# One core, attention and soft mixture: the first batch's casts, z parts, bounds and x times u stand at other places, and with them the last batch's v, three logits and the shifts

## Chip, cores and metric

The kernel runs on one core of a Trainium2 chip. The metric is the device time of one execution in microseconds, as the median of several.

## What is computed

Eight batches of relu-squared attention, followed by one soft mixture of experts over all tokens (cut to what matters):

```python
# u, v: (8, 2496, 256)   z: (8, 2496, 64)   f32
scores = (1/2496) * z @ z.transpose(0, 2, 1)
attn = np.maximum(scores, 0.0) ** 2
x = (u * (attn @ v)).reshape(19968, 256)
# phi: (256, 32)   w1: (8, 256, 1024)   w2: (8, 1024, 256)
logits = x @ phi
d = softmax(logits, axis=0)          # over tokens
slot_in = d.T @ x                    # 32 slots, 4 to an expert
slot_out[e] = relu(slot_in[e] @ w1[e]) @ w2[e]
out = softmax(logits, axis=1) @ slot_out
```

## The kernel before

**Halves.** A batch's 2496 queries are cut into five chunks, its keys into ten pieces of 256. One chunk with one piece is a half; a batch has 50, numbered through from 0. Matrices that need accuracy are held as two f16 parts, a high and a low one. For half k, `prepare(k)` issues: on TensorE the scores `sc` (z of the keys with z of the queries), on ScalarE relu and square into `r`, on GpSimd or ScalarE the cast `ph` (high part), on VectorE `pl`, which is r minus ph (low part). Since the scores are symmetric, VectorE also transposes `r` into `y`, and SyncE's DMAs carry it through DRAM, so that the mirrored half later only loads its `r`. Then `sums_halves` multiplies ph and pl by v into the accumulator `acc`, in two phases; between the phases stands `prepare` of a later half, and with it that half's scores. At the end of a chunk, `finish_chunk` multiplies the accumulator by u into `xg`.

**Order.** Every engine takes its instructions in the order in which the program writes them (`keep_in_program_order`). The order is written by hand: `landing[h]` holds what is issued with half h, and runs at the end of a `prepare`; tables say which step has which h. `work` holds the steps of the mixture for 1024 tokens (logits, exponentials, block transpositions, four shifts by DMA, the combine weights `c0` to `c3`); one is taken out with each half from the third piece of a chunk on.

**z, bounds, v.** The first 12 halves take their scores from raw f32 z. From half 14 on (halves 12, 13 are mirrored) they take z's two parts: `load_z` gives `split`, ScalarE's high part and then VectorE's low part. Scores consist of three pairs of matmuls: high with high, high keys with low queries, low keys with high queries. In batch 0, `FIRST_Z` says with which half each of z_1 to z_4 is split; scores 14 and 15 need z_1 and z_2, scores 16 and 17 z_1 and z_4, scores 18 first need z_3. For a later batch z's scale comes from its bounds: a square with a maximum per block (`sq`, into `tops`), summed over partitions by two small matmuls on TensorE (`add_bounds`), then `factors`. v's scale comes from its `energy` by `largest` (two VectorE instructions, into `few`) and `scale_v`, which begins with a small matmul on TensorE. v then is split like z (`v_high`, `v_low`).

**Opening.** Halves 0 and 1 are summed in f32, halves 2 and on in parts. In what comes first, GpSimd casts `r` of half 2 as soon as ScalarE has squared it, while VectorE runs `largest`; half 3 comes from an ordinary `prepare(3)` later.

Of the kernel before, what the change touches and what calls it, by code (L numbers as in the profile page):

```python
# [8 lines left out]
F32 = mybir.dt.float32  # L9
# [9 lines left out]
P = 128  # L19
B, S, D, DQK = 8, 2496, 256, 64  # L20
# [5 lines left out]
QC = 512  # L26
NQ = 5
# [4 lines left out]
NP = KT // 4  # L32
NBLK = 16
NRAW = 12
NW_OWN = 7
# [10 lines left out]
)  # L46
FIRST_MEETS = ((0, 1, 2, 3, 4), (1, 0, 2, 4, 3)) + MEETS[0][2:]

FIRST_Z = {8: 1, 10: 2, 11: 4, 13: 3}

RAW_SCORES = 12

FILL = 6, 3

WHOLE, KEEP = 2, 6

ON_ACT = 3, 5, 7

# [25 lines left out]
def attn_soft_moe_kernel(ctx, tc, uT, v, zz, zh, phi, ww, outT):  # L84
    nc = tc.nc

    pe, act, dve, sp, gp = (InOrder(tc, x) for x in (nc.tensor, nc.scalar, nc.vector, nc.sync, nc.gpsimd))
# [82 lines left out]
    def add_bounds(b, ps, js):  # L170
        ones_k = nc.const_aps.tensor(1.0, [P, P], F32)
        for h, rows in enumerate(HALF if b else [slice(0, P)]):
            pe.matmul(ps[:, h, js], ones_k[rows], tops[b % 2][rows, js], start=True, stop=True)

    def factors(b, ps, js):


        n2, by = (t[b % 2][:, js] for t in (norm2, z_by))
        total = ps[:, 0, js]
        if b:  # L180
            dve.tensor_reduce(n2, ps[:, :, js].rearrange("p h j -> p j h"), axis=AX.X, op=ALU.add)
            total = n2
        dve.tensor_scalar(bits(n2), bits(total), EVEN, None, op0=ALU.bitwise_and)
        dve.tensor_scalar(
            bits(by), bits(n2), EVEN, 1, op0=ALU.bitwise_xor, op1=ALU.logical_shift_right
        )
        dve.tensor_scalar_mul(by, by, 2.0**77)
# [29 lines left out]
    def largest(b):  # L217


        root, w = v_by[b % 2], few[b % 2]  # L220
        n2 = norm2[b % 2].unsqueeze(2).to_broadcast([P, NP, 2])
        dve.tensor_scalar(
            bits(root), bits(energy[b % 2]), 1, ROOT, op0=ALU.logical_shift_right, op1=ALU.bitwise_and
        )
        r2 = root.rearrange("p (j i) -> p j i", i=2)
        dve.tensor_tensor_reduce(
            r2, r2, n2, 1.0, 2.0**-120, op0=ALU.mult, op1=ALU.max, accum_out=w[:, 0:1]
        )

# [72 lines left out]
    own_w = moe.enter_context(tc.tile_pool(name="own_w", bufs=1))  # L302
    turns_sb = moe.enter_context(tc.tile_pool(name="turns_sb", bufs=4))
    att = ExitStack()
    wa = att.enter_context(tc.tile_pool(name="wa", bufs=2, side="right"))

    ut_ = {}
# [53 lines left out]
    middle, behind, stores, turning, casting, splitting = [], [], [], [], [], []  # L361

    def run(todo):
        now, todo[:] = todo[:], []
        for f in now:
            f()
# [99 lines left out]
    def prepare_first(k):  # L466

        r = wa.tile([P, 2, QC], F32, tag="r", name=f"r_{k}", bufs=4)
        pend[k] = hi, lo = high_low(k)
        ps, _ = early.pop(k)  # L470

        def parts(t):
            nc.gpsimd.tensor_copy(hi[:, t], r[:, t])
            return lambda: dve.tensor_sub(lo[:, t], r[:, t], hi[:, t])

        return lambda: relu(k, r, ps), lambda: act.activation(r, r, AF.Square), parts, lambda: stage(k, r)
# [119 lines left out]
    def await_(x, y):  # L596
        tc.add_manual_dep(
            x.ins, y.ins.name,
            mybir.DependencyInfo(mybir.DependencyClass.Sync, mybir.DependencyReason.DATA),
            reason="bank",  # L600
        )
# [64 lines left out]
    xg_ = {}  # L666

    def finish_chunk(b, ch, acc):
        j, _, n, t0 = ch
        ut = ut_.pop(t0)  # L670
        s = 0
        while s < n:
            q, o = divmod(t0 + s, 1024)
            w = min(n - s, 1024 - o)
            if q not in xg_:
                xg_[q] = wk.tile([P, 2, 1024], F32, tag="xg", name=f"xg_{q}")
            for c in (slice(0, 1), slice(1, 2)) if t0 + n == N else (slice(0, 2),):
                first = t0 == 0
                dve.scalar_tensor_tensor(
                    xg_[q][:, c, o : o + w], acc[:, c, s : s + w], out_by[b % 2][:, j : j + 1],  # L680
                    kept[0][:, c] if first else ut[:, c, s : s + w],
                    op0=ALU.mult, op1=ALU.add if first else ALU.mult,
                )
                if first:
                    dve.tensor_mul(xg_[q][:, :, 0:w], xg_[q][:, :, 0:w], ut)
            if o + w == 1024:
                work.extend(groups(q))
            s += w
# [23 lines left out]
    def groups(q):  # L712
# [3 lines left out]
        x = xg_[q]  # L716
# [134 lines left out]
        blocks = [lambda j=j, c=c: behind.append(lambda: turn_block(j, c)) for j in range(2) for c in range(2)]  # L851
# [3 lines left out]
        rest = lambda: None  # L855
        if q < NQG - 2:

            todo = [logits, ex, *blocks, e, *shifts[0:2], c0, *shifts[2:4], c1, c2]
            todo.append(lambda: (c3(), late.append(slot_sums)))
        else:  # L860


            todo = [rest, rest, logits, ex, lambda: behind.append(adding.pop(0)), rest]
            todo += [c0, c1, c2, c3, turn_e_whole, *[lambda i=i: turn_x_whole(i) for i in range(4)]]
            todo.append(lambda: late.append(last_slot_sums))
        return todo

    parts = {}
# [78 lines left out]

    def load_u(b, ch):
        _, _, n, t0 = ch
        ut = wa.tile([P, 2, QC], F32, tag="ut", name=f"ut_{t0}", bufs=1)  # L950
        q0 = t0 - b * S
        sp.dma_start(
            ut[:, :, :n], uT[b, :, q0 : q0 + n].rearrange("(c p) q -> p c q", p=P)
        )
        ut_[t0] = ut

    work = []
# [4 lines left out]
    for b in range(1, B):  # L962
        base, order = (b - 1) * 2 * NP * NQ, BLOCKS[b == B - 1]
        z_at = [28, 29, 30, 31, 39]
        v_from = [6, 7, 8, 9, 24, 25, 26, 31, 32, 33]
        v_sq = [17, 18, 19, 20, 28, 29, 30, 32, 33, 33]
        v_high = [43, 41, 41, 42, 42, 43, 44, 44, 45, 45]
        v_low = [47, 42, 43, 44, 45, 46, 48, 49, 50, 51]
        for i, (j, at) in enumerate(zip(order, z_at)):
            splits.setdefault(base + 9 + 2 * i, []).append((load_z, b, j, [base + 12 + 2 * i, base + at]))  # L970
        for i, (start, *steps) in enumerate(zip(v_from, v_sq, v_high, v_low)):
            splits.setdefault(base + start, []).append((load_v, b, i, [base + at for at in steps]))
        later[base + 23] = lambda b=b: add_bounds(b, next_acc(), slice(0, NP))
        later[base + 24] = lambda b=b: factors(b, accs[-1], slice(0, NP))
        later[base + 36] = lambda b=b: largest(b)
        later[base + 39] = lambda b=b: scale_v(b, ms_ps.tile([P, 2, 512], F32, tag="ms", name=f"mx_{b}"))
    landing, fetched = {}, set()
    accs = []

    def next_acc():  # L980

        accs.append(acc_ps.tile([P, 2, QC], F32, tag="acc", name=f"acc_{len(accs)}"))
        return accs[-1]
# [86 lines left out]
    for i in range(2, 2 * NP):  # L1070
        first_v[i](act if i in ON_ACT else dve)
    square2()
    low2 = [parts2(t) for t in range(2)]
    largest(0)
    sums_raw(1, acc_raw, 0, [1])
    scale_v(0, small)
    sums_raw(1, acc_raw, 1)
# [8 lines left out]
    dve.tensor_scalar(  # L1086
        raw_by[:, NP:], z_by[0][:, 1:2], z_by[0][:, 1:2], 2.0**-22, op0=ALU.mult, op1=ALU.mult
    )
    prepare(3)
    kept = [own_w.tile([P, 2, QC], F32, tag="own", name="kept", bufs=NW_OWN)]  # L1090
    landing_kept = lambda: act.activation(kept[0], acc_raw, AF.Identity, scale=2.0**22 / S**2)
    landing[KEEP] = [landing_kept]
# [1 line left out]
    for h, x in enumerate(halves):  # L1094
        if h < WHOLE:
            continue
        if x.begins:
            chunk = h // (2 * NP)
            acc = accs[chunk] if chunk < len(accs) else next_acc()
        last = len(halves) - h  # L1100
        transfers(h)
        if work and (x.at > 1 or last <= 20):
            work.pop(0)()
        weights(last)
        behind.extend(landing.pop(h, ()))
        ahead = [k for k in range(h + 2 + (h > CATCH), h + 3 + (h >= CATCH)) if k < len(halves) and k >= 3]
        split_first_v()
        run(casting)
        if not ahead and h < 1:
            run(middle)  # L1110
            run(turning)
            run(behind)
            sums_halves(h, acc, 1, sums_halves(h, acc, 0, None))
        elif ahead and not halves[ahead[0]].turned:
            turn = sums_halves(h, acc, 0, None)
            prepare(ahead.pop(0))
            sums_halves(h, acc, 1, turn)
        else:
            if ahead and not x.ends:
                prepare(ahead.pop(0))  # L1120
            elif not ahead:
                run(middle)
                run(casting)
                run(splitting)
                run(behind)
                between_last(3 - last)
            sums_whole(h, acc)
        if x.ends:
            finish_chunk(x.b, x.ch, acc)
        for k in ahead:  # L1130
            prepare(k)
        if h in FIRST_Z:
            z_splits.pop(FIRST_Z[h])()
        del pend[h]
# [314 lines left out]
```

## Time and profile before

| | us |
|---|---|
| median of 3 runs | 1269.56 |
| lowest, highest | 1269.4, 1270.18 |
| the profiled execution | 1269.41 |
| its span | 1267.6 |
| its mean granted TensorE clock | 0.987 of full speed |
| busy: VectorE | 1046.0 |
| busy: ScalarE | 841.9 |
| busy: GpSimd | 229.3 |
| tail with the outputs' DMAs at 417 GB/s | from about 1220 to the end |

The span runs from the first to the last instruction of the profiled execution; 1.8 us of its time lie outside. Busy times are sums over the span, so they say nothing of where an engine is needed; that is read from single stretches.

### The profile page before, as it was taken

The page shows a single profiled execution, that of the slowest core. Times are in us where ns is not written, and L with a number is a line of the kernel's source. Part 1 is how long each engine was busy: PE and PEld are TensorE (multiplying, and loading weights), DVE is VectorE, ACT ScalarE, POOL GpSimd, SP SyncE. Part 2 cuts the span into 40 slices and gives each one's busy share as a digit, 9 for nine tenths or more (in the row PEclk, how much of TensorE's full clock was granted, in tenths as well). Part 3 has the DMA queues.
Part 4 walks back from the last instruction along what each step waited for, and adds up shares of the span by engine and source line. Part 5 has one row for each costly group of instructions (what it writes and reads, how often), then busy time and mean ns, then how long its engine had stood idle before and what let it go on. Part 6 is the DMA issues. An engine that isn't in the chain of part 4 may idle for free.

```text
span 1267.6 us, 27769 instructions
## 1 busy us (share of the span) xinstructions
PE 1241.6 (98%) x10936; PEld 604.5 (48%) x10937; DVE 1046.0 (83%) x1468; ACT 841.9 (66%) x1143; POOL 229.3 (18%) x234
## 2 busy tenths in 40 slices
PE   9999999999999999999999999999999999999984
PEld 3444454444544444445544444444444455445752
DVE  7988898779978889788987888788987789776563
ACT  7877765767666766577656776577666777564552
POOL 2211032201311032110311123110321113110100
PEclk9999999999999999999999999999999999999995
DMA  6778469773878748784787758786587848989769
GB/s 197 244 211 277 170 190 303 232 238 119 240 263 270 240 126 274 244 235 163 213 276 218 268 149 244 256 255 210 156 277 230 267 142 239 277 278 328 280 272 376
DMA packets 136690, 299.28 MB, mean 236 GB/s; under 512 B 17904, under 2 KB 38896, under 8 KB 124656
## 3 DMA queue, kind: packets, MB, share of 16 engines
q1 hardware_dynamic: 136560, 297.51, 74.0%
q8 instruction: 86, 1.41, 0.5%
q14 instruction: 44, 0.36, 0.1%
HBM read 162.43 MB, written 113.77 MB: 218 GB/s over the span
## 4 chain that ended last, share of the span: by engine, by line
PE 93%; ACT 2%; DVE 2%; DMA 1%; issue 1%; POOL 0%; ACTq 0%; DVEq 0%; POOLq 0%
PE acc L80 76%; PE sc L80 11%; PE lg L80 3%; DMA outT<-ot 1%; PE pf L80 1%; ACT r L80 1%; ACT ot L80 1%; DVE pl L80 1%; PE h L80 1%; PE po L80 0%; DVE y L80 0%; PE acc_raw L80 0%; DVE v L80 0%; DVE xg L80 0%; PE xt L80 0%
## 5 line engine op out<-in xcount | busy, mean ns | idle before, releaser
L80 PE MATMUL acc<-ph,v 64*128 64x512 f16 (+4 forms) x5004 | 923.7, 368 | 0.4 <-POOLq L80 0.3
L80 PEld LDWEIGHTS <-v 64*128 64x128 f16 (+1 forms) x7506 | 467.7, 95 | 521.3 <-issue 38.6
L80 PE MATMUL acc<-pl,v 64*128 64x512 f16 (+5 forms) x2502 | 597.9, 368 | 2.3 <-DVE pl L80 2.3
L80 DVE TENSOR_TENSOR pl<-r,ph 128x1024 f16<-128x1024 f32 (+1 forms) x428 | 475.7, 1123 | 35.0 <-ACT ph L80 25.6
L80 POOL CAST ph<-r 128x1024 f16<-128x1024 f32 (+1 forms) x210 | 224.4, 1072 | 942.7 <-ACT r L80 693.8
L80 ACT ACTIVATE r<-sc 128x1024 f32<-128x1024 f32 (+1 forms) x233 | 220.3, 946 | 234.5 <-PE sc L80 231.9
L80 DVE STREAM_TRANSPOSE y<-r 128x1024 f32<-128x1024 f32 x160 | 198.3, 1239 | 68.9 <-ACT r L80 65.0
L80 ACT ACTIVATE r<-r 128x1024 f32<-128x1024 f32 (+1 forms) x243 | 239.0, 983 | 7.7
L80 ACT CAST ph<-r 128x1024 f16<-128x1024 f32 (+1 forms) x180 | 172.0, 963 | 98.3 <-PE acc L80 60.0
L80 PE MATMUL sc<-z,z 64*128 64x512 f16 x912 | 123.9, 376 | 0.0
L80 PEld LDWEIGHTS <-z 64*128 64x128 f16 x1380 | 69.7, 94 | 72.1 <-DVE z L80 0.3
L80 DVE SCALAR_TENSOR_TENSOR xg<-acc,out_by,ut 128x1024 f32<-128x1024 f32 (+7 forms) x56 | 50.6, 926 | 17.7 <-PE acc L80 17.4
L80 DVE SCALAR_TENSOR_TENSOR v<-vr,v_by,v 128x512 f16<-128x512 f32 (+1 forms) x81 | 60.6, 750 | 0.0
L80 ACT ACTIVATE v<-vr,v_by 128x512 f16<-128x512 f32 (+1 forms) x81 | 53.8, 707 | 7.6 <-DVE v_by L80 7.6
L80 DVE STREAM_TRANSPOSE yd<-r 128x512 f32<-128x512 f32 x36 | 25.5, 709 | 31.2 <-ACT r L80 29.8
L80 PE MATMUL sc<-z 64*128 64x512 f16 (+1 forms) x468 | 50.6, 321 | 0.0
L80 DVE STREAM_TRANSPOSE y<-xg 128x512 f32<-128x512 f32 x72 | 49.4, 686 | 0.0
L80 ACT ACTIVATE vq<-vr 128x512 bf16<-128x512 f32 x73 | 45.5, 623 | 3.6 <-DMA vr<-in_v 3.3
L80 DVE COPY ot<-pf 128x1024 f32<-128x1024 f32 (+2 forms) x21 | 24.1, 1147 | 18.1 <-PE pf L80 14.6
L80 DVE TENSOR_TENSOR pl<-rd,ph 128x512 f16<-128x512 f32 x36 | 24.7, 686 | 14.9 <-ACT ph L80 14.9
L80 ACT COPY ot<-pf 128x1024 f32<-128x1024 f32 (+2 forms) x21 | 20.0, 951 | 22.8 <-PE pf L80 16.4
L80 DVE SCALAR_TENSOR_TENSOR z<-zr,z_by,z 128x512 f16<-128x512 f32 x35 | 25.8, 737 | 0.0
(193 smaller groups left out, 555.9 us busy)
## 6 DMA issues: line engine op xcount, KB each, us to landing
turned<-y SPq DMA_DIRECT2D x320, 256.0 KB, 5.5
r<-turned SPq DMA_DIRECT2D x76, 1024.0 KB, 7.3
xt<-y SPq DMA_DIRECT2D x288, 72.0 KB, 3.9
vr<-in_v SPq DMA_DIRECT2D x80, 256.0 KB, 4.9
outT<-ot SPq DMA_DIRECT2D x17, 1024.0 KB, 7.0
ut<-in_uT SPq DMA_DIRECT2D x31, 512.0 KB, 6.2
lent<-yd SPq DMA_DIRECT2D x144, 64.0 KB, 3.3
rd<-lent SPq DMA_DIRECT2D x36, 256.0 KB, 4.0
```

The source lines that it names most:

```text
L80: return lambda *a, **k: self.tc.keep_in_program_order(f(*a, **k))
```

## The change

It does six things, all of them in the order of instructions.

1. Opening: ScalarE takes relu and square of half 3 directly behind the square of half 2, ahead of v's high parts. GpSimd's first cast waits for the second instruction of `largest`, and half 3's two casts follow half 2's.
2. `FIRST_Z`: z_1, z_2, z_4 and z_3 are split with halves 10, 11, 13 and 15, where 8, 10, 11 and 13 stood. The first chunk's product of x and u is not issued in `finish_chunk` but with half 17; the first u lies in another buffer.
3. Batch 1's five squares of the bounds stand with halves 21 to 25 (12, 14, 16, 18, 20 before), its `add_bounds` with half 26 (23 before), its `factors` with 27 (24).
4. Some of the last batch's low parts of v come up to four halves earlier.
5. In batches 1, 3 and 5 the logits are taken out of `work` one half earlier.
6. `c0` stands behind all four shifts, no longer between the second and the third, so the last two shifts come earlier.

```diff
-FIRST_Z = {8: 1, 10: 2, 11: 4, 13: 3}
+FIRST_Z = {10: 1, 11: 2, 13: 4, 15: 3}
+FIRST_U = 17
+EDGE = 21
...
-        def parts(t):
-            nc.gpsimd.tensor_copy(hi[:, t], r[:, t])
+        def parts(t, behind_of=None):
+            cast = gp.tensor_copy(hi[:, t], r[:, t])
+            if behind_of is not None:
+                await_(cast, behind_of)
             return lambda: dve.tensor_sub(lo[:, t], r[:, t], hi[:, t])
...
                 if first:
-                    dve.tensor_mul(xg_[q][:, :, 0:w], xg_[q][:, :, 0:w], ut)
+                    landing.setdefault(FIRST_U, []).append(
+                        lambda x=xg_[q][:, :, 0:w]: dve.tensor_mul(x, x, ut)
+                    )
...
-            todo = [logits, ex, *blocks, e, *shifts[0:2], c0, *shifts[2:4], c1, c2]
+            todo = [logits, ex, *blocks, e, *shifts, c0, c1, c2]
...
-        v_low = [47, 42, 43, 44, 45, 46, 48, 49, 50, 51]
+        v_low = [47, 42, 43, 44, 45, 46, 48, 49, 50, 51] if b < B - 1 else [46, 42, 43, 43, 44, 44, 45, 45, 46, 47]
         for i, (j, at) in enumerate(zip(order, z_at)):
-            splits.setdefault(base + 9 + 2 * i, []).append((load_z, b, j, [base + 12 + 2 * i, base + at]))
+            bound = 21 + i if b == 1 else 12 + 2 * i
+            splits.setdefault(base + 9 + 2 * i, []).append((load_z, b, j, [base + bound, base + at]))
...
-        later[base + 23] = lambda b=b: add_bounds(b, next_acc(), slice(0, NP))
-        later[base + 24] = lambda b=b: factors(b, accs[-1], slice(0, NP))
+        add_at = 26 if b == 1 else 23
+        later[base + add_at] = lambda b=b: add_bounds(b, next_acc(), slice(0, NP))
+        later[base + add_at + 1] = lambda b=b: factors(b, accs[-1], slice(0, NP))
...
     square2()
-    low2 = [parts2(t) for t in range(2)]
-    largest(0)
+    relu3, square3, parts3, stage3 = prepare_first(3)
+    relu3()
+    square3()
+    found = largest(0)
+    low2, low3 = ([parts(t, found if parts is parts2 and t == 0 else None) for t in range(2)] for parts in (parts2, parts3))
     sums_raw(1, acc_raw, 0, [1])
...
-    prepare(3)
+    run(turning)
+    for f in low3:
+        f()
+    stage3()
...
-        if work and (x.at > 1 or last <= 20):
+        if work and (x.at > 1 or last <= 20 or (0 < x.b < B - 1 and h % (2 * NP * NQ) == EDGE)):
             work.pop(0)()
```

**The opening on GpSimd and ScalarE.** GpSimd before: the casts of half 2 (`ph_241`), then those of half 3 (`ph_287`) and of half 4.

```order
L473 CAST ph_241<-r_240 128x512 [waits Activation_49]
L473 CAST ph_241<-r_240 128x512
L80 CAST ph_287<-r_283 128x512 [waits Activation_49]
L80 CAST ph_287<-r_283 128x512
L80 CAST ph_318<-r_311 128x512 [waits PE_49,Activation_49]
```

GpSimd now, the same place; half 3's cast is `ph_262`:

```order
L84 CAST ph_241<-r_240 128x512 [waits DVE_49,Activation_49]
L84 CAST ph_241<-r_240 128x512
L84 CAST ph_262<-r_261 128x512 [waits Activation_49]
L84 CAST ph_262<-r_261 128x512
L84 CAST ph_318<-r_311 128x512 [waits PE_49,Activation_49]
```

ScalarE before, from the square of half 2 (`r_240`) on; `r_283` is half 3:

```order
L80 ACTIVATE r_240<-r_240 128x1024
L80 ACTIVATE v_2_127<-vr_2_134,v_by_89 128x256 [waits DMAHW5_49,DVE_49]
L80 ACTIVATE v_2_127<-vr_2_134,v_by_89 128x256
L80 ACTIVATE v_2_127<-vr_3_135,v_by_89 128x2x256
L80 ACTIVATE r_283<-sc_236,raw_by 128x1024 [waits PE_49]
L80 ACTIVATE r_283<-r_283 128x1024 [waits Activation_49]
```

ScalarE now; `r_261` is half 3:

```order
L84 ACTIVATE r_240<-r_240 128x1024
L84 ACTIVATE r_261<-sc_236,raw_by 128x1024 [waits PE_49]
L84 ACTIVATE r_261<-r_261 128x1024 [waits Activation_49]
L84 ACTIVATE v_2_127<-vr_2_134,v_by_89 128x256 [waits DMAHW5_49,DVE_49]
L84 ACTIVATE v_2_127<-vr_2_134,v_by_89 128x256
L84 ACTIVATE v_2_127<-vr_3_135,v_by_89 128x2x256
```

The first cast has a wait on VectorE more, and half 3's relu and square have moved ahead of v_2's three high parts.

**VectorE about halves 14 to 17.** Before, from z_4's low part on: `pl` and `y` of half 14 (`r_725`), a square of the bounds, `pl` and `y` of half 15 (`r_774`), and z_3's low part.

```order
L80 SCALAR_TENSOR_TENSOR z_4_125<-cw,z_by_85,z_4_125 128x512 [waits Activation_49]
L80 TENSOR_TENSOR pl_736<-r_725,ph_735 128x512 [waits PE_49,Activation_49]
L80 TENSOR_TENSOR pl_736<-r_725,ph_735 128x512 [waits Activation_49]
L80 STREAM_TRANSPOSE y_741<-r_725 128x2x16x32 [waits DMAHW3_49,DMAHW4_49,DMAHW2_49,DMAHW1_49]
L80 ISA sq_0_743,tops_82<-zr_0_533 128x512 [waits DMAHW6_49]
L80 ISA tops_82 128x1
L80 TENSOR_TENSOR pl_785<-r_774,ph_784 128x512 [waits PE_49,Activation_49]
L80 TENSOR_TENSOR pl_785<-r_774,ph_784 128x512 [waits Activation_49]
L80 STREAM_TRANSPOSE y_741<-r_774 128x2x16x32
L80 SCALAR_TENSOR_TENSOR z_3_124<-cw,z_by_85,z_3_124 128x512 [waits Activation_49]
L80 TENSOR_TENSOR pl_834<-r_823,ph_833 128x512 [waits PE_49,Pool_49]
L80 TENSOR_TENSOR pl_834<-r_823,ph_833 128x512 [waits Pool_49]
```

Now, from `y` of half 14 (`r_722`) on; `r_769` is half 15, `r_818` half 16, `r_865` half 17:

```order
L84 STREAM_TRANSPOSE y_738<-r_722 128x2x16x32 [waits DMAHW3_49,DMAHW4_49,DMAHW2_49,DMAHW1_49]
L84 TENSOR_TENSOR pl_780<-r_769,ph_779 128x512 [waits PE_49,Activation_49]
L84 TENSOR_TENSOR pl_780<-r_769,ph_779 128x512 [waits Activation_49]
L84 STREAM_TRANSPOSE y_738<-r_769 128x2x16x32
L84 SCALAR_TENSOR_TENSOR z_4_125<-cw,z_by_85,z_4_125 128x512 [waits Activation_49]
L84 TENSOR_TENSOR pl_829<-r_818,ph_828 128x512 [waits PE_49,Pool_49]
L84 TENSOR_TENSOR pl_829<-r_818,ph_828 128x512 [waits Pool_49]
L84 STREAM_TRANSPOSE y_834<-r_818 128x2x16x32 [waits DVE_49]
L84 TENSOR_TENSOR pl_876<-r_865,ph_875 128x512 [waits PE_49,Activation_49]
L84 TENSOR_TENSOR pl_876<-r_865,ph_875 128x512 [waits Activation_49]
L84 STREAM_TRANSPOSE y_834<-r_865 128x2x16x32
L84 SCALAR_TENSOR_TENSOR z_3_124<-cw,z_by_85,z_3_124 128x512 [waits DMAHW6_49,Activation_49]
```

z_4 has moved behind `y` of half 15, to where z_3 stood, and z_3 behind `y` of half 17; the square is gone from here.

TensorE before, at scores 16 (`sc_824`), between the two phases of half 14's sums:

```order
L80 MATMUL acc_667<-pl_736,v_4_128 128x512
L80 LDWEIGHTS z_4_125
L80 MATMUL sc_824<-z_1_122,z_4_125 128x512 [waits Activation_49]
L80 LDWEIGHTS z_4_125
L80 MATMUL sc_824<-z_1_122,z_4_125 128x512
L80 LDWEIGHTS z_4_125
L80 MATMUL sc_824<-z_1_122,z_4_125 128x512
L80 LDWEIGHTS z_4_125
L80 MATMUL sc_824<-z_1_122,z_4_125 128x512
L80 LDWEIGHTS z_4_125
```

TensorE now, the same place (`sc_819`):

```order
L84 MATMUL acc_664<-pl_733,v_4_128 128x512
L84 LDWEIGHTS z_4_125 [waits Activation_49]
L84 MATMUL sc_819<-z_1_122,z_4_125 128x512 [waits PE_49]
L84 LDWEIGHTS z_4_125
L84 MATMUL sc_819<-z_1_122,z_4_125 128x512
L84 LDWEIGHTS z_4_125
L84 MATMUL sc_819<-z_1_122,z_4_125 128x512
L84 LDWEIGHTS z_4_125
L84 MATMUL sc_819<-z_1_122,z_4_125 128x512
L84 LDWEIGHTS z_4_125 [waits DVE_49]
```

The weights for the first pair now wait for ScalarE's z_4 and those for the third pair for VectorE's.

**TensorE and VectorE at the bounds of batch 1.** TensorE before, at the end of scores 26 (`sc_1193`):

```order
L80 LDWEIGHTS z_3_124
L80 MATMUL sc_1193<-z_2_123,z_3_124 128x512
L80 LDWEIGHTS z_3_124
L80 MATMUL sc_1193<-z_2_123,z_3_124 128x512
L80 MATMUL acc_1207<-tops_82,const-float32-1.0 128x5 [waits DVE_49]
L80 MATMUL acc_1207<-tops_82,const-float32-1.0 128x5
```

TensorE now, at the end of scores 29 (`sc_1331`), which the second phase of half 26's sums follows:

```order
L84 LDWEIGHTS z_2_123
L84 MATMUL sc_1331<-z_2_123 128x256
L84 LDWEIGHTS z_2_123
L84 MATMUL sc_1331<-z_2_123 128x256
L84 MATMUL acc_1348<-tops_82,const-float32-1.0 128x5 [waits DVE_49]
L84 MATMUL acc_1348<-tops_82,const-float32-1.0 128x5
L84 LDWEIGHTS v_6_129 [waits Pool_sequencer_49]
L84 MATMUL acc_1035<-ph_1219,v_6_129 128x512
```

VectorE now, `y` of half 28 (`r_1285`) and what follows it; `y_1248<-xg_662` is a block's transposition:

```order
L84 TENSOR_TENSOR pl_1270<-r_1235,ph_1269 128x1024 [waits PE_49,Pool_49]
L84 STREAM_TRANSPOSE y_1246<-r_1285 128x2x16x32 [waits Activation_49]
L84 STREAM_TRANSPOSE y_1248<-xg_662 128x4x4x32
L84 ISA sq_4_1298,tops_82<-zr_4_850 128x512 [waits DMAHW2_49,DVE_49]
L84 ISA tops_82 128x1
L84 TENSOR_TENSOR pl_1315<-r_1285,ph_1314 128x1024 [waits PE_49,Pool_49]
```

The two small matmuls over `tops` have moved by three halves, and the last square stands behind two transpositions on VectorE, where before the second of those was followed by `pl`.

## Rows read from the trace of the kernel before

**Rows 1.** The first part of the page: busy time of an engine, its share of the span, and its number of instructions.

```profile
PE 1241.6 (98%) x10936; PEld 604.5 (48%) x10937; DVE 1046.0 (83%) x1468; ACT 841.9 (66%) x1143; POOL 229.3 (18%) x234
```

**Rows 2.** The fourth part of the page, its row by engine: what share of the span the chain of waits that ended last spends on each.

```profile
PE 93%; ACT 2%; DVE 2%; DMA 1%; issue 1%; POOL 0%; ACTq 0%; DVEq 0%; POOLq 0%
```

**Rows 3.** TensorE by stretches of the span: from and to, length, busy time and instructions, granted clock as a share of full speed, busy share of the DMA engines, GB/s.

```profile
700.00:1000.00 300.00, 300.00 (x2615) 1.00 0.75 230
...
1230.00:1240.00 10.00, 5.34 (x62) 0.79 1.02 417
1240.00:1250.00 10.00, 7.04 (x56) 0.50 1.01 419
```

**Rows 4.** What TensorE waited for over the whole span: us in total, number of waits, the longest.

```profile
PE acc L80 <- DVE pl L80: 2.3, 6, 0.8
PE acc L80 <- DVE few L80: 0.7, 1, 0.7
PE acc L80 <- POOLq L80: 0.3, 1, 0.3
```

**Rows 5.** The timeline of the opening and, for the last two of VectorE's rows, of a later batch: start and duration in us, engine, line and operation, with the idle time ahead of it and what ended it in brackets. First VectorE, then GpSimd, then TensorE.

```profile
13.87 0.44 DVE L80 TENSOR_SCALAR v_by<-energy 128x10 int32<-128x10 int32 x1
14.34 0.51 DVE L80 CUSTOM_DVE_ANT_1 v_by<-v_by,norm 128x10 f32<-128x10 f32 x1
...
20.60 1.06 DVE L80 TENSOR_TENSOR pl<-r,ph 128x512 f16<-128x512 f32 x1 [0.29 <-POOL ph L80]
...
129.73 0.17 DVE L80 TENSOR_SCALAR v_by<-energy 128x10 int32<-128x10 int32 x1
129.93 0.17 DVE L80 CUSTOM_DVE_ANT_1 v_by<-v_by,norm 128x10 f32<-128x10 f32 x1
...
13.66 1.17 POOL L473 CAST ph<-r 128x512 f16<-128x512 f32 x2 [9.95 <-ACT r L80]
19.95 1.17 POOL L80 CAST ph<-r 128x512 f16<-128x512 f32 x2 [5.11 <-ACT r L80]
...
15.01 0.46 PE L80 MATMUL acc<-ident,few 128*128 128x128 f32 x2 [0.74 <-DVE few L80]
```

**Rows 6.** The timeline of halves 11 to 14: VectorE, then TensorE.

```profile
50.06 1.22 DVE L80 TENSOR_TENSOR xg<-xg,ut 128x1024 f32<-128x1024 f32 x1
51.20 1.28 DVE L80 TENSOR_TENSOR pl<-r,ph 128x512 f16<-128x512 f32 x2
52.41 0.74 DVE L80 SCALAR_TENSOR_TENSOR z<-cw,z_by,z 128x512 f16<-128x512 f32 x1
...
48.28 0.38 PE L80 MATMUL acc<-pl,v 128*128 128x512 f16 x1 [0.19 <-DVE pl L80]
...
51.94 0.39 PE L80 MATMUL acc<-pl,v 64*128 64x512 f16 x2 [0.80 <-DVE pl L80]
...
52.80 0.83 PE L80 MATMUL sc<-z,z 64*128 64x512 f16 x6
```

**Rows 7.** The timeline of halves 14 to 17: the scores 16 and 18 on TensorE, the casts of half 15 on ScalarE, and the work of half 15 and the z piece behind it on VectorE.

```profile
59.27 0.83 PE L80 MATMUL sc<-z,z 64*128 64x512 f16 x6
...
65.78 0.81 PE L80 MATMUL sc<-z,z 64*128 64x512 f16 x6
...
59.04 1.14 ACT L80 CAST ph<-r 128x512 f16<-128x512 f32 x2
...
59.69 1.29 DVE L80 TENSOR_TENSOR pl<-r,ph 128x512 f16<-128x512 f32 x2 [0.20 <-ACT ph L80]
60.91 1.24 DVE L80 STREAM_TRANSPOSE y<-r 128x1024 f32<-128x1024 f32 x1
62.07 0.71 DVE L80 SCALAR_TENSOR_TENSOR z<-cw,z_by,z 128x512 f16<-128x512 f32 x1
```

**Rows 8.** The timeline of halves 19 and 20: `pl` of half 20 on VectorE, then TensorE's first read of `pl` of half 19 and of half 20.

```profile
75.72 1.24 DVE L80 TENSOR_TENSOR pl<-r,ph 128x512 f16<-128x512 f32 x2
...
74.08 0.38 PE L80 MATMUL acc<-pl,v 128*128 128x512 f16 x1 [0.26 <-DVE pl L80]
...
76.67 0.38 PE L80 MATMUL acc<-pl,v 128*128 128x512 f16 x1
```

**Rows 9.** The timeline about the bounds of batch 1: the last square of the bounds, and the work of half 28, on VectorE; the sum over the bounds and scores 29 on TensorE.

```profile
82.16 0.68 DVE L80 CUSTOM_DVE_ANT_0 sq<-zr 128x512 bf16<-128x512 f32 x1
...
97.77 1.24 DVE L80 STREAM_TRANSPOSE y<-r 128x1024 f32<-128x1024 f32 x1
98.93 0.67 DVE L80 STREAM_TRANSPOSE y<-xg 128x512 f32<-128x512 f32 x1
...
88.48 0.28 PE L80 MATMUL acc<-tops,const-float32-1.0 64*128 64x5 f32 x4
...
97.68 0.49 PE L80 MATMUL sc<-z 64*128 64x256 f16 x6
```

**Rows 10.** What TensorE waited for between 1036 and 1070 us (total, number, longest), and two of VectorE's rows from the timeline there.

```profile
PE acc L80 <- DVE pl L80: 1.0, 3, 0.5
...
1041.30 2.06 DVE L80 TENSOR_TENSOR pl<-r,ph 128x1024 f16<-128x1024 f32 x1
...
1044.77 0.82 DVE L80 SCALAR_TENSOR_TENSOR v<-vr,v_by,v 128x512 f16<-128x512 f32 x1
```

More of the change, by code (lines that the diff above doesn't have):

```diff
@@ L225, in largest @@
         r2 = root.rearrange("p (j i) -> p j i", i=2)
-        dve.tensor_tensor_reduce(
+        return dve.tensor_tensor_reduce(
             r2, r2, n2, 1.0, 2.0**-120, op0=ALU.mult, op1=ALU.max, accum_out=w[:, 0:1]
@@ L949, in load_u @@
         _, _, n, t0 = ch
-        ut = wa.tile([P, 2, QC], F32, tag="ut", name=f"ut_{t0}", bufs=1)
+        place, n_bufs = (wa, 1) if t0 else (own_w, NW_OWN)
+        ut = place.tile([P, 2, QC], F32, tag="ut" if t0 else "own", name=f"ut_{t0}", bufs=n_bufs)
         q0 = t0 - b * S
```

## The prediction

> **What bounds the kernel now.** I read the page's shares first: TensorE is busy 1241.6 of 1267.6 us [rows 1], and the chain that ended last runs through it for 93% [rows 2]. The windows then show where the rest lies: from 700 to 1000 TensorE is busy every microsecond; only the tail from 1230 on is loose, where the granted clock falls from 1.00 to 0.50 [rows 3]. So in the stream nothing but TensorE counts, and a microsecond of waiting there moves the end by a microsecond. The table of TensorE's waits says how little there is to win: 2.3 us for `pl` (the low half of the probabilities) in six waits, 0.7 for `few`, 0.3 for GpSimd's turn mark [rows 4]. Outside the tail that is 3.3 us. The timeline prints a wait about 0.17 short, because a matmul's printed span overlaps the next (0.61 printed, 0.43 from start to start), so I count 0.19 as 0.36.
>
> The change saves no work: each engine issues the same instructions in another order. The question is, for each moved instruction, whether a TensorE wait goes and whether another comes.
>
> **The opening.** The two instructions of `largest` take 0.44 and 0.51 us while GpSimd casts, and 0.17 each in a later batch [rows 5]: if the cast comes after them, `few` is ready 0.61 earlier and TensorE's wait of 0.74 at 15.01 nearly goes. GpSimd's cast now waits for `largest`, and behind it on GpSimd stand its second part and half 3's two, for which VectorE's `pl` wait. But two casts of half 3 (1.17 us together, at 19.95 now) then fall between VectorE's subtractions and v's low parts of half 2, since ScalarE squares half 3 in its own gap before v. At 20.60 a subtraction that shares its time with a GpSimd cast took 1.06 instead of 0.68, 0.38 more [rows 5]. Two such meetings cost 0.76 on a chain whose second `pl` ends now just as TensorE wants it. The wait of 0.33 at 20.00 goes too, its cast being done early. Sum −0.61 + 0.76 − 0.33 = **−0.2**; bounds −1.0 (both waits go, no meeting bites) and +0.5 (VectorE is held for both casts in full).
>
> The Trainium skill's page "SBUF — State Buffer", section "Who interferes with whom", says that VectorE and GpSimd share one pair of ports as an exclusive lock, that a VectorE instruction with two SBUF inputs meets a GpSimd instruction that reads SBUF, and that the one issued first makes the other wait in full. By that rule the two meetings would be worth 1.17 and the opening +0.2, so it speaks against this part of the change. The trace agrees that they hinder each other (1.06 against 0.68), but with a smaller price.
>
> **Halves 11 to 14.** Before, z_1's low part stands ahead of `pl` of half 11 and x times u (1.22) ahead of `pl` of half 12; TensorE waits 0.19 at 48.28 and 0.80 at 51.94 [rows 6]. Both are gone afterwards: 0.36 + 0.97 = −1.3. But TensorE then comes to scores 14 at 51.5 instead of 52.80, and its third pair, 0.43 later, needs z_2's low part. Ahead of that stood x times u (1.22); afterwards `pl` of half 13 stands there instead (1.28, as `pl` at 51.20), so it still ends at 53.2. TensorE starts about 0.14 after a releaser's end (`few` is read out by 14.87, TensorE starts at 15.01) [rows 5], so the new wait is 53.35 − 51.9 = +1.4. Sum **+0.1**; bounds −0.4 and +0.6.
>
> **z_4 and z_3.** This is the largest term. Before, z_4's low part is done long before its use: scores 16 run at 59.27 with no wait [rows 7]. Afterwards it takes the place in VectorE's order that z_3 has now: behind `pl` and the transposition `y` of half 15, which is two halves ahead of the sums. The times of that place: ScalarE's casts of half 15 begin at 59.04, `pl` at 59.69, `y` at 60.91, the z piece at 62.07, ending 62.78 [rows 7]. Nothing there can be sooner, since scores 15 must pass relu, square, cast, `pl` and `y`. Scores 16 stand one half (two phases and a score, 3.24) behind scores 15. They start at 59.27, their third pair at 59.70, and it waits until 62.92: **+3.2**. Behind it all of TensorE's sums wait, since it takes its instructions in order. ScalarE's high part of z_4, behind the two casts (59.04 and 1.14) and worth some 0.7 like the low part, makes the first pair wait some 1.6 of these 3.2.
>
> z_3 moves the same way, behind `y` of half 17, with scores 18 one half behind scores 17: the same offsets, **+3.2**. z_3 ends at 62.78 now and is first read at 65.78 [rows 7]; that cover of 3.0 us is gone. Bounds for each: 2.6 (VectorE has its bounds squares out of the way and the transposition runs sooner) and 3.5.
>
> **x times u at half 19.** It now stands ahead of `pl` of half 20, which starts at 75.72 and reaches TensorE with 0.3 us to spare (its first part, half of the 1.24, ends near 76.35, and TensorE reads it at 76.67) [rows 8]. It costs 1.22; the square of the bounds that stood ahead of `pl` of half 19 goes, so that wait (0.26 printed, 0.42) shrinks by half, to 0.2, as a cast meets the first subtraction. New wait 1.22 − 0.3 = 0.9. Sum 0.9 − 0.2 = **+0.7**; bounds −0.3 (VectorE has caught up during TensorE's long waits and absorbs the product) and +1.0.
>
> **Bounds of batch 1.** The last square of the bounds is done at 82.85 now, 5.6 us before TensorE's small sum `acc<-tops` at 88.48. Afterwards that sum stands directly behind scores 29, which start at 97.68 and end 0.33 later, and the square behind `y` of half 28 (97.77, 1.24) and a block's transposition (98.93, 0.67) [rows 9]. Two starts fix it: the block ends near 99.5, the square takes 0.68 and its read-out 0.07, so TensorE goes on at about 100.3 instead of 98.0: **+2.2**, with 1.7 and 2.5 as bounds. The squares for halves 21 to 24 find VectorE with over 1.7 us before TensorE's reads, so they cost nothing; without that cover each would cost its 0.68.
>
> **Last batch.** Three waits for `pl` make 1.0 us printed [rows 10]. The first stays: that `pl` takes 2.06 beside a cast at 1041.30. The other two lie behind low parts of v (one at 1044.77, 0.82) that now come ahead of it. Printed they make 0.5, from start to start 0.8, and a fourth too short to be printed adds 0.2: **−1.0**; bounds −1.7 (the first goes too) and −0.3.
>
> **The rest, at nothing.** Logits one half earlier in three batches: VectorE has 4 us there before TensorE needs it, and `xg` is finished a microsecond ahead; uncovered, up to 1 us each. `c0` (1.4 us on VectorE) behind the shifts takes as much from halves 55 and 56 as it puts on 57 and 58; eight DMAs of the last two shifts pass some loads of mirrored halves on SP's queue, which arrive 2 us or more early. I take 0 with ±0.5.
>
> **Sum.** −0.2 + 0.1 + 3.2 + 3.2 + 0.7 + 2.2 − 1.0 = +8.2 us. The profiled execution took 1269.41, so 1277.6; the median of the runs is 0.15 above it. I say 1277.6.
>
> **Rivals.**
> - *The moved pieces come in time* (faster). If VectorE's z and bounds pieces were finished when TensorE reads them, only what is won remains: the opening's 0.9, halves 11 to 14's 1.3, half 19's 0.4, the last batch's 1.0, together 3.6: 1265.8. It decides once the three new waits together are below 1 us. For it speaks only that VectorE idles in places; against it, that it takes its instructions in the order listed and the chain of half 15 alone is 3.2 us too long.
> - *Waits cancel* (no measurable change). It needs two of the three big waits to be absent: 8.2 − 3.2 − 3.2 = +1.8, 1271.2. Against it: z_4 and z_3 stand in the same position.
> - *One of the big waits is absent or half as long*: +5, 1274.5. Bounds squares or `y` running sooner would do it.
> - *The clock falls in the long waits* (slower still). The one fall in the trace comes after 1230 to 1240, where TensorE was busy 5.34 of 10 us [rows 3]; waits of up to 0.8 us in the stream brought none. If half speed followed each wait for about its own length, half of 8.6 is added: 1281.9. Scores 16 and 18 break their waits, since two pairs run between the high part and the low part. The Trainium skill's "TensorE: Matmul & The Clock Gate", section "HAM oscillation — how this bites in real kernels", says that long idle gaps of TensorE bring the lower clock; no row of this trace shows it inside the stream.
>
> **How the numbers follow.** Forecast 0.73 (its own range 1275.5 to 1279.5, from the bounds added as independent); clock 0.09; one wait absent 0.10; waits cancel 0.04; pieces in time 0.04. A measurement of this kernel tells about 0.2%, 2.5 us, from no change, so 1267.0 to 1272.1 is "same". Faster 0.04, same 0.04, slower 0.92. The range takes in "one wait absent" and the nearer part of the clock's case: 1273.8 to 1280.5.
>
> **What the profile after would show.** TensorE's waits get rows for `z` on ScalarE and VectorE near 59 and 66, 1.6 and 1.5 us each, and one for `tops` of about 2.2 near 105. VectorE's z pieces stand behind `y`. The wait of 0.80 before `pl` near 51 is gone and one for z_2 of 1.4 stands in its place. The first instruction of `largest` takes 0.17, and GpSimd's first cast begins after it. In the last batch one `pl` wait of 0.55 is left. I would be wrong if scores 16 start without waiting, or if TensorE's clock falls below 1.00 before 1230.

## The result and the profile after

The changed kernel takes 1278.18 us (median of 6, 1277.71 to 1280.87) against 1269.74 for the kernel before (6 runs); the ratio is 1.0072, with a 95% interval of 1.0062 to 1.0082. The forecast was 1277.6, and slower. The profiled execution took 1277.73, its span grew from 1267.6 to 1275.9.

What TensorE waited for over the whole span (us in total, number, longest), beside [rows 4]:

```profile
PE sc L84 <- DVE z L84: 4.0, 3, 1.4
PE sc L84 <- ACT z L84: 3.0, 2, 1.6
PE acc L84 <- DVE tops L84: 2.0, 1, 2.0
PE acc L84 <- DVE pl L84: 1.5, 3, 0.7
...
PE acc L84 <- DVE v L84: 0.3, 1, 0.3
PE acc L84 <- DVE few L84: 0.2, 1, 0.2
```

Two kinds of wait are new, for `z` and for `tops`, 9.0 us printed. The waits for `few` and for GpSimd's turn mark have shrunk or gone, and `pl` has 1.5 us in three waits where it had 2.3 in six.

**z parts.** TensorE's timeline at scores 14 (third pair), scores 16 (first, then third pair) and scores 18 (the same); the idle time ahead stands in brackets:

```profile
53.13 0.39 PE L84 MATMUL sc<-z,z 64*128 64x512 f16 x2 [1.23 <-DVE z L84]
...
60.77 0.61 PE L84 MATMUL sc<-z,z 64*128 64x512 f16 x4 [1.42 <-ACT z L84]
...
62.74 0.61 PE L84 MATMUL sc<-z,z 64*128 64x512 f16 x2 [1.37 <-DVE z L84]
...
71.73 0.61 PE L84 MATMUL sc<-z,z 64*128 64x512 f16 x4 [1.63 <-ACT z L84]
...
73.70 0.39 PE L84 MATMUL sc<-z,z 64*128 64x512 f16 x2 [1.37 <-DVE z L84]
```

VectorE and ScalarE ahead of scores 16: `pl` and `y` of half 15 and z_4's low part, then z_4's high part.

```profile
59.60 1.29 DVE L84 TENSOR_TENSOR pl<-r,ph 128x512 f16<-128x512 f32 x2 [0.80 <-ACT ph L84]
60.81 1.24 DVE L84 STREAM_TRANSPOSE y<-r 128x1024 f32<-128x1024 f32 x1
61.97 0.71 DVE L84 SCALAR_TENSOR_TENSOR z<-cw,z_by,z 128x512 f16<-128x512 f32 x1
...
59.99 0.72 ACT L84 ACTIVATE z<-cw,z_by 128x512 f16<-128x512 f32 x1
```

The rows are those of [rows 7] a tenth earlier, with z_4 in z_3's place: it ends at 62.68, and TensorE's third pair goes on at 62.74. From start to start the five waits lose 1.40, 1.58, 1.53, 1.79 and 1.53 us.

**Granted clock.** TensorE by stretches: from and to, length, busy time and instructions, granted clock, DMA share, GB/s.

```profile
59.00:60.70 1.70, 0.35 (x4) 1.00 0.00 0
60.70:62.70 2.00, 0.61 (x4) 0.85 0.00 0
62.70:65.40 2.70, 2.66 (x14) 0.50 0.90 187
65.40:70.00 4.60, 4.60 (x44) 0.99 0.58 151
...
71.70:73.70 2.00, 0.61 (x4) 1.00 0.62 246
73.70:80.00 6.30, 6.29 (x49) 1.00 0.69 169
```

Behind the wait of scores 16, TensorE runs 2.7 us at a granted clock of 0.50 (1.2 GHz in place of 2.4); seven starts follow each other there at some 0.43 us instead of 0.22, which costs 1.4 us. Behind the equally long wait of scores 18 the clock stays at 1.00.

**Bounds of batch 1.** VectorE, then TensorE, at scores 29 and the sum over `tops`:

```profile
105.66 1.24 DVE L84 STREAM_TRANSPOSE y<-r 128x1024 f32<-128x1024 f32 x1
106.83 0.67 DVE L84 STREAM_TRANSPOSE y<-xg 128x512 f32<-128x512 f32 x1
107.42 0.65 DVE L84 CUSTOM_DVE_ANT_0 sq<-zr 128x512 bf16<-128x512 f32 x1
...
105.66 0.49 PE L84 MATMUL sc<-z 64*128 64x256 f16 x6
...
108.14 0.39 PE L84 MATMUL acc<-tops,const-float32-1.0 64*128 64x5 f32 x4 [1.98 <-DVE tops L84]
```

VectorE ends the last square's read-out at 108.08; the sum waits from 105.99 to 108.14, 2.15 us from start to start.

**Opening.** VectorE (the row of L80 is of the kernel before), GpSimd, TensorE; `few`, v's low part and the second `pl` are what TensorE waits for. The rows `acc_raw` are its fourth product with `vr`, now and (L80) before.

```profile
14.10 0.17 DVE L84 TENSOR_SCALAR v_by<-energy 128x10 int32<-128x10 int32 x1
14.31 0.17 DVE L84 CUSTOM_DVE_ANT_1 v_by<-v_by,norm 128x10 f32<-128x10 f32 x1
...
16.51 1.57 DVE L84 SCALAR_TENSOR_TENSOR v<-vr,v_by,v 128x256 f16<-128x256 f32 x2
...
16.89 0.87 DVE L80 SCALAR_TENSOR_TENSOR v<-vr,v_by,v 128x256 f16<-128x256 f32 x2
...
14.62 1.17 POOL L84 CAST ph<-r 128x512 f16<-128x512 f32 x2 [10.91 <-DVE few L84]
15.95 1.86 POOL L84 CAST ph<-r 128x512 f16<-128x512 f32 x2 [0.15 <-ACT r L84]
...
12.48 1.98 PE L84 MATMUL acc_raw<-r,vr 128*128 128x512 f32 x4
...
12.28 1.98 PE L80 MATMUL acc_raw<-r,vr 128*128 128x512 f32 x4
...
14.63 0.46 PE L84 MATMUL acc<-ident,few 128*128 128x128 f32 x2 [0.17 <-DVE few L84]
...
17.40 0.39 PE L84 MATMUL acc<-ph,v 64*128 64x512 f16 x2 [0.27 <-DVE v L84]
...
18.75 0.39 PE L84 MATMUL acc<-pl,v 64*128 64x512 f16 x2 [0.21 <-DVE pl L84]
```

The two instructions of `largest` now take 0.17 each, ahead of the first cast. But half 3's casts take 1.86 in place of 1.17 and v's low parts beside them 1.57, where they took 0.87 before. From the fourth `acc_raw` to scores 4 TensorE takes 9.93 us (12.48 to 22.41), where it took 10.32 (12.28 to 22.60): 0.39 less. That it stands 0.20 later at 12.48 is not shown to come from the change: in the 14 traces of all kernels here this row starts at 12.07 to 13.57, and at 12.93 in a second execution of the changed kernel (e11).

**Half 20 and the last batch.** The product of x and u and the `pl` behind it on VectorE, and TensorE's wait:

```profile
82.95 1.18 DVE L84 TENSOR_TENSOR xg<-xg,ut 128x1024 f32<-128x1024 f32 x1
84.06 2.48 DVE L84 TENSOR_TENSOR pl<-r,ph 128x512 f16<-128x512 f32 x4
...
84.79 0.38 PE L84 MATMUL acc<-pl,v 128*128 128x512 f16 x1 [0.71 <-DVE pl L84]
```

The last batch's one wait for `pl` on TensorE, and the first of its logits:

```profile
1053.34 0.36 PE L84 MATMUL acc<-pl,v 64*128 64x448 f16 x2 [0.58 <-DVE pl L84]
...
1058.90 1.09 PE L84 MATMUL lg<-xg,phi_sb 64*32 64x256 f32 x32
```

**Where the time went.** Both traces issue the same scores in the same order, and the logits shown here have not moved among them, so a row's start in one less its start in the other tells what has been lost up to there:

| up to | before | after | difference | in this stretch |
|---|---|---|---|---|
| scores 4 | 22.60 | 22.41 | −0.19 | later start +0.2, opening −0.4 |
| scores 14 | 52.80 | 51.31 | −1.49 | −1.3 |
| scores 15 | 56.03 | 55.95 | −0.08 | z_2 +1.4 |
| scores 17 | 62.51 | 66.92 | +4.41 | z_4 +3.1, half clock +1.4 |
| scores 19 | 68.59 | 76.09 | +7.50 | z_3 +3.3, turn mark −0.2 |
| first logits | 82.26 | 90.38 | +8.12 | half 20 +0.6 |
| scores 30 | 100.38 | 110.75 | +10.37 | bounds +2.25 |
| logits | 874.30 | 884.20 | +9.90 | −0.5 |
| logits | 1109.63 | 1118.20 | +8.57 | last batch −1.3 |
| end of the span | 1267.6 | 1275.9 | +8.3 | tail −0.3 |

### The profile page after: what moved, and what is told of

Its sections match the earlier page's. It is cut to its first block, busy times and chain, and to the rows that moved or that the text cites. A ratio compares the mean times of both kernels' runs of the same rounds, so it can differ in the third digit from the quotient of the medians.

```text
span 1275.9 us, 27781 instructions
## 1 busy us (share of the span) xinstructions
PE 1242.6 (97%) x10936; PEld 603.5 (47%) x10937; DVE 1043.3 (82%) x1468; ACT 841.4 (66%) x1143; POOL 237.1 (19%) x234
## 4 chain that ended last, share of the span: by engine, by line
PE 91%; DVE 3%; ACT 2%; DMA 2%; issue 1%; POOL 0%; SPq 0%; ACTq 0%; DVEq 0%; POOLq 0%
PE acc L84 74%; PE sc L84 11%; PE lg L84 3%; ACT r L84 1%; PE pf L84 1%; DMA outT<-ot 1%; DVE pl L84 1%; ACT ot L84 1%; DVE y L84 1%; PE h L84 1%; PE po L84 1%; DMA vr<-in_v 0%; DMA cw<-in_zz 0%; DVE v L84 0%; ACT ph L84 0%
## 5 line engine op out<-in xcount | busy, mean ns | idle before, releaser
L84 POOL CAST ph<-r 128x1024 f16<-128x1024 f32 (+1 forms) x212 | 233.4, 1104 | 953.4 <-ACT r L84 720.8
```

What stands on the lines that cost most here:

```text
L84: return lambda *a, **k: self.tc.keep_in_program_order(f(*a, **k))
```

## The experiments

Each kernel was timed beside the kernel before on the same chip; that one took 1269.5 to 1269.7 in all three groups of runs.

**e1, z back.** The changed kernel with

```diff
-FIRST_Z = {10: 1, 11: 2, 13: 4, 15: 3}
+FIRST_Z = {8: 1, 10: 2, 11: 4, 13: 3}
```

> The changed kernel with the four z parts at their old places (x times u at half 17 and the late bounds stay). Theory, that the waits for z_4 and z_3 and a stretch of half clock behind the first are the loss: 4.5 and 3.1 us go, the 1.4 at z_2 goes, 0.35 for half 11's subtraction returns, so 1269.5. Rival, that VectorE is late as a whole and the wait only shows up at z: the loss comes back at the next read, at half 19 or at the bounds, and the time stays above 1273.

Measured 1270.85 (1268.87 to 1271.65), ratio 1.0007 (0.9998 to 1.0016). All waits for `z` are gone and nothing has taken their place at half 19: the rival falls. The median is 1.3 us above the forecast; what can account for it stands in the trace behind the wait for `tops` (TensorE's row, then stretches):

```profile
99.87 0.28 PE L84 MATMUL acc<-tops,const-float32-1.0 64*128 64x5 f32 x2 [1.98 <-DVE tops L84]
...
97.60:100.00 2.40, 0.42 (x8) 1.00 1.08 391
101.40:104.60 3.20, 3.20 (x18) 0.50 1.02 344
```

Here the half clock has come behind the bounds' wait, at least 3.2 us of it and 1.6 us lost, where the changed kernel's own profile had 1.00.

**e2, bounds back.** The changed kernel with

```diff
-            bound = 21 + i if b == 1 else 12 + 2 * i
+            bound = 12 + 2 * i
...
-        add_at = 26 if b == 1 else 23
+        add_at = 23
```

> The changed kernel with batch 1's bounds and their sum at the old places. Theory: the 2.2 us wait for tops goes, the squares ahead of half 19's subtraction cost about 0.4 again, 1276.2. Rival, that the wait for tops is covered by what follows: no change, 1278.2.

Measured 1276.81 (1275.57 to 1277.61), ratio 1.0051 (1.0039 to 1.0064). The wait for `tops` is gone, and the rival falls: all five runs lie below those of the changed kernel. In its profile both z waits are followed by half clock, one stretch more than in the changed kernel's, which can be why the time is 0.6 above the forecast:

```profile
63.10:66.60 3.50, 3.50 (x20) 0.52 0.97 229
...
74.00:76.60 2.60, 2.45 (x12) 0.50 0.86 181
```

**e3, both back.** Both edits together, so that the opening, the product, the last batch, the logits and the shifts are left.

> The changed kernel with z and bounds both at their old places: the opening, x times u at half 17, the last batch, logits and shifts are left. Theory: terms -0.2 (opening), -1.0 (half 12), +0.7 (half 19), -1.3 (last batch), -0.5 (in between), so 1267.5. Rival, that what is left is worth nothing: 1269.6.

Measured 1267.61 (1266.72 to 1268.07), ratio 0.9982 (0.9974 to 0.9991). The edits that are left win 2.0 us; z and bounds together cost some 10.5 (8.44 and 2.01, each against the kernel before timed beside it).

**e5, z_3 and z_4 swapped**, in the kernel before:

```diff
-FIRST_Z = {8: 1, 10: 2, 11: 4, 13: 3}
+FIRST_Z = {8: 1, 10: 2, 11: 3, 13: 4}
```

> The kernel before, with z_3 and z_4 changing places (z_3 with half 11, z_4 with half 13) and nothing else. Theory: TensorE waits 3.1 us at scores 16, as in the changed kernel, the wait of 0.24 at 62.94 goes, and where half clock follows the wait 1.4 to 1.7 more: 1272.5 without, 1274.0 with. Rival, that the wait in the changed kernel needs the other edits too: below 1271.

Measured 1273.31, ratio 1.0031 (1.0019 to 1.0043); its runs lie at 1272.5 to 1272.6 (three) and 1274.0 to 1274.6 (three). The profiled one is of the lower three, with a clock of 1.00 behind the wait, and shows scores 16:

```profile
61.02 0.61 PE L80 MATMUL sc<-z,z 64*128 64x512 f16 x4 [1.41 <-ACT z L80]
...
62.99 0.39 PE L80 MATMUL sc<-z,z 64*128 64x512 f16 x2 [1.37 <-DVE z L80]
```

One place in VectorE's order is enough for the 3.1 us; the rest of the change isn't needed. The step of 1.4 to 2 us between the two threes has the size of a stretch of half clock; that the upper three had one was not traced.

**e8, work in the waits.** The changed kernel with matmuls that nobody reads:

```diff
+        idle = ms_ps.tile([P, 2, 512], F32, tag="ms", name=f"idle_{k}") if k in (16, 18) else None
+        def busy():
+            if idle is not None:
+                for i in range(6):
+                    pe.matmul(idle[:, i % 2], ones[:, 0:P], ones, start=True, stop=True)
+        busy()
...
             for i, (kl, ql) in enumerate(((0, 0), (0, 1), (1, 0))):
+                if i == 2:
+                    busy()
...
+        if b == 1:
+            for i in range(9):
+                pe.matmul(ps[:, i % 2], ones[:, 0:P], ones, start=True, stop=True)
```

> The changed kernel with extra matmuls on ones, whose result nobody reads, written into the three long waits: 6 ahead of the first pair and 6 ahead of the third pair of scores 16 and of scores 18, 9 ahead of the small sum over tops. Theory, that TensorE's idling in the waits brings the stretches of half clock: the waits stay as long, filled with work, the granted clock stays 1.00 until the tail, and the kernel with more work is faster than the changed one, 1276.4 against 1278.2, without executions near 1280.8. Rival, that the clock falls for another cause: 1278.2 and the same stretches; or that the extra work costs its 7 us: 1285.

Measured 1277.03 (1276.01 to 1278.21), ratio 1.0060 (1.0047 to 1.0073). One of TensorE's rows and its stretches:

```profile
59.97 1.48 PE L84 MATMUL idle<-const-bfloat16-1.0 128*128 128x512 bf16 x6
...
58.00:62.00 4.00, 4.00 (x31) 1.00 0.00 0
62.00:66.00 4.00, 4.00 (x32) 1.00 0.58 122
66.00:74.00 8.00, 7.78 (x58) 1.00 0.75 250
105.00:108.00 3.00, 3.00 (x25) 1.00 1.01 289
```

With 33 matmuls more, the kernel is some 1.2 us faster than the changed one's first six runs, and seven of that kernel's ten runs (e11's four included) lie above the slowest of these five. In the profiled execution the clock stays at 1.00 until the tail, also where the DMA share is 1.01: it was the idling that brought the half clock. 1277.0 is 0.6 above the forecast, inside the spread of its own runs; scores 4 stand at 23.09 here in place of 22.41, so this execution came 0.7 late to where the edits begin.

**e11, the changed kernel again.**

> The changed kernel once more, for its granted clock: theory, three waits of 2 us and more, each of which brings a stretch of half clock in some executions and not in others, 1276.4 with none and 1.3 to 1.6 more for each, so times from 1276.5 to 1281 in steps. Rival, that the stretch at 62.7 stands in every execution: the same trace, all times within 0.5 of 1278.

Measured 1280.69 (1278.71 to 1281.09, 4 runs), ratio 1.0084 (1.0070 to 1.0098). This execution's stretches:

```profile
63.00:66.30 3.30, 3.30 (x18) 0.51 0.97 225
...
74.00:80.00 6.00, 5.93 (x28) 0.50 0.72 175
...
108.00:112.00 4.00, 2.02 (x26) 1.00 0.95 336
```

Half clock stands behind both z waits, 6 us of it behind the second, and none behind the bounds' wait. The same program thus takes about 1276.4 plus what the clock takes, 1.4 to 4.3 in the profiles seen. The rival falls; and this median lies above the whole range of the forecast (1273.8 to 1280.5), into which the first six runs came.

**e6, the last batch alone**, in the kernel before:

```diff
-        v_low = [47, 42, 43, 44, 45, 46, 48, 49, 50, 51]
+        v_low = [47, 42, 43, 44, 45, 46, 48, 49, 50, 51] if b < B - 1 else [46, 42, 43, 43, 44, 44, 45, 45, 46, 47]
```

> The kernel before with only the last batch's low parts of v moved. Theory: of its four waits for a subtraction the last three go, 1.0 to 1.3 us, 1268.4. Rival, that VectorE delays something else there: no change, 1269.6.

Measured 1268.19 (1267.42 to 1270.22), ratio 0.9991 (0.9982 to 1.0000). In its trace TensorE's scores fall from −0.1 to −1.4 us against before between 1008 and 1062, 0.34 of it at the logits.

**e7, the opening alone**, in the kernel before (the edits to `largest`, `prepare_first` and the opening).

> The kernel before with only the opening changed. Theory: few is ready 0.6 us earlier, two new waits of 0.4 us each come behind it for the low part of v and the second subtraction, and the 0.5 at GpSimd's turn mark goes: -0.2 to -0.5, 1269.2. Rival, by the rule that a cast blocks VectorE for its whole length: slower by 0.2 or more.

Measured 1269.30 (1268.45 to 1270.86), ratio 0.9998 (0.9989 to 1.0006): nothing that can be measured. The traces say why. From the fourth `acc_raw` to scores 4, TensorE takes 10.32 and 10.42 us with the old opening in the two executions that wait for `few` (before, e5), but 9.34 in the three that don't (e6, e9, e12). With the new opening it takes 9.93 and 9.85 with such a wait (the changed kernel's own profile, this one), and 9.52 or 9.53 in the seven traces without. So the new opening wins 0.4 to 0.6 where the execution waits for `few`, and loses 0.2, the rival's amount, where it doesn't.

**e9, logits and shifts alone**, in the kernel before (the edits to `todo` and to the condition on `work`).

> The kernel before with only the shifts ahead of c0 and the logits of three batches one half earlier. Theory: about 0.1 at each of four or five small waits for a subtraction two halves into the batches goes, -0.3 to -0.5 in the trace between 140 and 1000, 1269.2. Rival, that it only moves the same work: 0.0.

Measured 1269.35 (1268.84 to 1270.78), ratio 1.0000 (0.9991 to 1.0009). Its trace gains 0.3 us at the logits of the three batches (0.11, 0.13 and 0.05), as the changed kernel's does. Waits of 0.5 and less at 857 to 875 then take more than that back in the profiled execution; such waits stand in e7's trace too, at 417, 418 and 713, far behind its edits, so they need not be e9's.

**e12, the product alone**, in the kernel before (the edits to `finish_chunk` and `load_u`).

> The kernel before with only the first chunk's product of x and u moved to half 17. Theory: the wait of 0.97 at half 12 goes and one of 0.9 at half 20 comes, with the square still ahead of half 19 0.4 stays: 1269.5, no change that can be measured. Rival, that VectorE has room at half 19: 1268.6.

Measured 1269.56 (1268.90 to 1270.78), ratio 1.0001 (0.9992 to 1.0009). The wait at half 12 has gone, scores 14 stand 0.9 us earlier, and half 20 takes it back:

```profile
76.64 0.38 PE L80 MATMUL acc<-pl,v 128*128 128x512 f16 x1 [0.71 <-DVE pl L80]
```

**e4, a better table.** The changed kernel with

```diff
-FIRST_Z = {10: 1, 11: 2, 13: 4, 15: 3}
+FIRST_Z = {9: 1, 10: 2, 11: 4, 13: 3}
...
-FIRST_U = 17
+FIRST_U = 12
...
-            bound = 21 + i if b == 1 else 12 + 2 * i
+            bound = 20 + i if b == 1 else 12 + 2 * i
```

> The changed kernel with z_1 at 9, z_2 at 10, z_4 at 11, z_3 at 13, x times u at half 12, and batch 1's squares at halves 20 to 24 with their sum still at 26. Theory: no wait for z_4, z_3 or tops, 0.2 for z_2, none for half 20's subtraction: 1266.0. Rival, that moved work on VectorE always meets some read: 1268 to 1270.

Measured 1266.21 (1264.95 to 1267.12), ratio 0.9969 (0.9958 to 0.9981): it beats both kernels. What TensorE still waits for `pl` ahead of 1200:

```profile
PE acc L84 <- DVE pl L84: 0.8, 2, 0.6
```

No wait for `z` or `tops` is left.

**e10, e4 with v_9's low part late again** (the last entry of the last batch's `v_low` 51 in place of 47).

> The candidate of before (z parts at 9, 10, 11, 13, x times u at 12, squares at 20 to 24) with the last batch's v_9 low part at 51 again. Theory: the subtraction in the last batch that takes 2.06 starts 0.7 earlier, ahead of GpSimd's cast, and TensorE's wait of 0.74 goes: 1265.5. Rival, that the cast then waits and the next subtraction is late instead: 1266.2 as without it.

Measured 1265.88 (1264.90 to 1266.91), ratio 0.9969 (0.9959 to 0.9980). The `pl` that took 2.06 [rows 10] now starts ahead of the cast:

```profile
1038.37 1.22 DVE L84 TENSOR_TENSOR pl<-r,ph 128x1024 f16<-128x1024 f32 x1
```

TensorE waits for no `pl` between 1000 and 1100 any more, and its scores there gain 0.74 us on e4's. The time is not told apart from e4's: other small waits near 1170, of 0.5 and 0.4, stand in this execution.

## Why the prediction was right, and where its terms were off

- **z_4, z_3 (+3.2 each): right.** 3.11 and 3.32 were measured, in two parts each, as worked out from the place of z_3 in the kernel before. e5 shows it alone, e1 that it goes.
- **Halves 11 to 14 (+0.1): right**, −1.3 and +1.4 as forecast. The moved product paid for one wait with another.
- **Half 20 (+0.7): right**, +0.6; e12 shows the trade it belongs to, −0.9 at half 12 and +0.9 here.
- **Bounds (+2.2): right**, +2.25.
- **The opening (−0.2): the size near, in part by luck.** The −0.19 at scores 4 is a start 0.20 later and a gain of 0.39. The meetings cost 0.70 here, where 0.76 was put in, but they hit v's low parts, not `pl`. The term rests on the wait for `few` in one execution: three of the five traces with the old opening have none, and against those the new opening loses 0.2 (e7). By the lock of "SBUF — State Buffer" (section "Who interferes with whom") in the Trainium skill, each of the two meetings would take a whole cast, an estimate of 1.17 in all. VectorE lost 0.70, and GpSimd's casts 0.69 themselves (1.86 against 1.17); the prediction counted no wait on GpSimd's side.
- **The last batch (−1.0):** −1.3. Of the three printed waits for `pl` the first stayed, and the other two went with the one too short to be printed, as said: 0.97 together. The third of a microsecond more was in the logits: from the first of them to the sums behind them they took 2.23 us before (1049.42 to 1051.65) and 1.89 now (1058.90 to 1060.79), where `xg`, which they read, was finished at 1049.97 with v's low part ahead of it, after their start, and is finished at 1058.33 now, ahead of it. The traces of e3, e4 and e6, which have the same v edit, gain the same 0.34 there. No run moved `xg` alone, so that it is `xg` is argued, not shown.
- **The clock: the rival that was given 0.09 came true in part.** A clock below 1.00 before 1230 was named as a sign of being wrong, and it came, at 62. The step that failed was the reading that pairs of matmuls in the middle of a wait keep the clock up. (The one fall in the trace before came inside the stretch 1230 to 1240, as its 0.79 says, not after it.) The rival priced three stretches at 4.3 together; this profile has one, 1.4, and e11's has two, 4.3. That 1277.6 was met to 0.6 us is therefore in part luck, and e11's 1280.69 missed it by 3.1: the 1.4 of the clock is not in the sum, and −0.5 in the middle, −0.3 in the last batch and −0.3 in the tail are not either. With the clock at 1.00 the kernel would take about 1276.4, 1.2 below the forecast and still inside its own range.
- **The rest (0 ± 0.5):** −0.5 in the middle. Of this, 0.3 is at the logits of the three batches, as in e9's trace. The other 0.2 (at 458) is gained on the kernel before by e5, e6 and e12 too, which change nothing there; it belongs to that kernel's one execution.

## What to carry to other kernels

When engines take their instructions in order, a moved instruction ends where the chain ahead of its new place ends: look that place up in the old trace, add the moved duration, and compare with the reader's time; here it gave four waits (z_2, z_4, z_3 and the bounds) to within 0.12 us. A high and a low part that one engine reads in turn are each a deadline, and a product moved out of one tight place needs a second place with room for its whole length. Where TensorE bounds a kernel, count for waits like these (2.15 us, 3.1 us) the half clock that can follow them, and time such a kernel in many executions, since its times come in steps. Before a gain is priced from a wait, see whether a second execution has the wait: the one for `few` stood in two of five.

## What the hardware showed that was not expected

Waits of 3.1 us with four matmuls in the middle were followed by half clock in some executions and by none in others of the same program: behind scores 18, none in the changed kernel's own profile and 6 us in e11's. A wait of 2.15 us in one piece was followed by it in e1, and in neither profile of the changed kernel. The stretches shown are 2.6 to 6 us long and cost 1.3 to 2.6 us each. The wait of 1.4 us at z_2 had none behind it in its four profiles (the changed kernel's, e2, e8, e11). Filling the waits with useless matmuls (e8) took the stretches away and made the kernel faster with more work. This goes beyond the Trainium skill's "TensorE: Matmul & The Clock Gate" (section "HAM oscillation — how this bites in real kernels"), by which long idle gaps bring the lower clock: here the gap was cut in two, and it still did.
